# A delta-rule attention with a top-2 expert layer on one core: TensorE's order written out, outputs one unit behind, two triangular solves on VectorE

## The chip, the cores and the metric

The kernel runs on one core of a Trainium2 chip. The metric is device time in microseconds (us), lower is better. The core has a matrix engine (TensorE, PE in the profile, with its weight loads as PEld), a vector engine (VectorE, DVE), a scalar engine (ScalarE, ACT), a general engine (GpSimd, POOL) and an engine that starts transfers (SyncE, SP). Each engine works through its own instructions in order. Matrix results land in PSUM, which has eight banks; VectorE and ScalarE read them out.

## What is computed

The first half is a linear attention with a state matrix for each of 4 x 8 heads, 768 steps long, head size 40:

```
for t in range(S):
    y[:, :, t] = einsum('bhd,bhde->bhe', rt, state)
    Sa = einsum('bhde,bhe->bhd', state, at)
    state = state * wt[:, :, None, :] - einsum('bhd,bhe->bhde', Sa, bt) + einsum('bhd,bhe->bhde', vt, kt)
```

The second half sends each of the 3072 rows (all heads side by side, 320 wide) to two of eight experts. The choice is by noisy logits, `x@w_gate + log1p(exp(x@w_noise))*noise`; an expert is `relu(x@w1)@w2` with a hidden width of 1024, and the two results are summed with softmax weights.

## The kernel before

**Attention** is done in chunks of 64 steps. A unit n is one chunk cc of one half p of the batch (2 batch entries x 8 heads), so there are 12 x 2 = 24 units; p alternates. Four units (two chunks, both halves) are a group g; there are six groups.

What does not need the state is made for a whole group. `prepA` (L457, once for each p) builds the running product of w with a scan (L466), its inverse (Ln and Exp on ScalarE, a correction on VectorE, L469-475), scales b and a with it (L489, L491), splits them into two f16 parts (`pack`, L425) and sends them through DRAM into the operand stacks `st_ab` (L492-496; five buffers, SAB). NG (L477) has six buffers and is read by a transposition on TensorE at the end of each unit (`pgm`, L673). `prepC` (L505) does the same for k. `scoresL` (L520) multiplies a against b, ScalarE empties the block (L527), and four transfers write the strictly lower parts to DRAM (`scr`, L529). `tsolve` (L531) reads them as 128 small 32 x 32 systems, X, into one buffer (L534), masks them with a multiply (L535) and inverts them in 30 steps of one multiply and one add (L541, L542) on one engine, POOL for all six groups (`TPOOL`); the result is split into f16 parts th (L544, L545) and goes back to DRAM. `fetchB` (L564) brings a unit's share into dT.

A unit's `chain` (L620) is the serial part: split the state into `sfs` (L605, L606) and stack it (sE), add a·sE to W, split W (w1), apply dT (Q), copy Q to q, add the cross term to W, split again (w2), apply dT again (U), copy U twice into `vu` and once into `Ut` (L642-644), and form the new state Sst (L652). `pre` (L576) makes the next unit's key scores and first W, `blocks` (L585) its b and k blocks kb. `outp` (L654) forms the unit's output: turn U, two score blocks masked to P (L665), Y, and a scaling by the transposed NG (L676). `m.logits` (L102) then writes the output rows to DRAM, turns them, and multiplies with the gate weights. After 8, 16, 20, 22 and 24 units `route` (L127) ranks the rows by expert, and `scatter` (L158) writes a list entry for each row and choice with a POOL transfer (L162); the first are held until the last solve is issued (`m.sg`).

**Experts** follow (L273 and L295 hold their matmuls): for each expert a gather of its rows (L241), two matmul stages in three f32r parts, and a POOL transfer that adds to the output (L297).

A scheduler in the compiler orders each engine's instructions by a simulated time and a priority. `burst` (L433) ties the matmuls of one block together; which block comes after which on TensorE is the scheduler's choice. `chain` has a high priority (PRIO). Two zero matmuls are issued ahead of Q (`warm`, L568, ND).

PSUM: psc one bank, pst one, pacc three (W, Q, U, S, Y), pt two, pp one.

Of the kernel before, what the change touches and what calls it, by code (L numbers as in the profile page):

```python
# [41 lines left out]
class Moe:  # L42
    def __init__(s,nc,tc,ctx,aps):
        s.nc,s.tc=nc,tc
        s.wgn_d,s.nz_d,s.w1_d,s.w2_d,s.out_d=aps
# [56 lines left out]
    def logits(s,n,xt,ps,tag,bufs=(1,1)):  # L102

        nc=s.nc
        s.xw=nc.sync.dma_start(s.xd[n>=NA][128*n:128*n+128],xt)
# [267 lines left out]

class Att:
    PSC=1; PACC=3; PT=2; PPB=1
    def __init__(s,nc,tc,ctx,aps):
# [9 lines left out]
        s.psa=ec(tc.tile_pool(name="psa",bufs=1,space=PSUM)); s.psb=ec(tc.tile_pool(name="psb",bufs=1,space=PSUM)); s.ps=ec(tc.tile_pool(name="ps",bufs=1,space=PSUM))  # L386
        s.consts()
    def consts(s):
# [26 lines left out]
        nc.gpsimd.affine_select(out=s.tri,in_=s.tri,pattern=[[-1,32],[1,32]],base=0,channel_multiplier=0,compare_op=ALU.is_gt,fill=0.0)
# [41 lines left out]
    def prepA(s,p,g):  # L457
        nc=s.nc; FM=s.aps[0]
# [7 lines left out]
        nc.vector.tensor_tensor_scan(fl(Gx),w,fl(s.d1),0.0,op0=ALU.mult,op1=ALU.add)  # L466
# [415 lines left out]
```

## Time and profile before

| what | us |
|---|---|
| median of 3 runs (lowest, highest) | 1027.19 (1023.14, 1027.94) |
| the profiled execution: device time | 1021.33 |
| the profiled execution: span | 1019.5 |
| PE busy | 767.5 (75%) |
| POOL busy | 521.4 (51%) |
| DVE busy | 492.1 (48%) |
| ACT busy | 396.1 (39%) |

The span is from the first to the last instruction. A busy share is a mean over stages: the attention ends near 572 and the experts begin near 606. In a timeline row stand start, duration, engine, line, operation, output<-inputs, shapes, count, and in brackets how long the engine had been idle and what ended that. A row of busy times by stretch gives for each engine the busy time and the number of instructions, then the clock that TensorE was granted (1.00 is full), the mean busy share of the DMA engines, and GB/s.

### The profile page before, as it was taken

What the parts mean: (1) busy time and instruction counts of PE and PEld (TensorE: products, weight loads), DVE (VectorE), ACT (ScalarE), POOL (GpSimd) and SP (SyncE); (2) the same over time, 40 slices, a digit from 0 to 9 for tenths busy, and PEclk for the clock granted to TensorE, in tenths of its full rate; (3) what the DMA queues carried; (4) which work ended last, traced back from release to release, by engine and by line L of the source; (5) the groups of instructions that cost most, each with busy time, mean ns of one, the idle gap of its engine ahead of it and who ended that gap; (6) DMA issues with size and microseconds to landing.
All of it is one profiled execution on the core that took longest, in us unless ns stands there. A gap on an engine that the chain in (4) does not pass through costs nothing.

```text
span 1019.5 us, 25178 instructions
## 1 busy us (share of the span) xinstructions
PE 767.5 (75%) x10506; PEld 681.2 (67%) x10506; DVE 492.1 (48%) x961; ACT 396.1 (39%) x816; POOL 521.4 (51%) x678
## 2 busy tenths in 40 slices
PE   0110117687877687899799379999999999999995
PEld 0110116576666576787688259899999989999995
DVE  9329525355567556447355542643434334443430
ACT  2213213354444344554454322543434334343421
POOL 6259979237967728818874335133333333333313
PEclk9999999797778787999899779999999999999998
DMA  3799963478479557655355843426262525262303
GB/s 96 188 203 226 242 172 90 116 197 225 127 193 241 146 121 204 175 152 146 96 120 148 272 119 68 131 49 150 49 150 49 150 49 149 50 149 51 36 7 40
DMA packets 135264, 136.21 MB, mean 134 GB/s; under 512 B 67392, under 2 KB 114948, under 8 KB 135060
## 3 DMA queue, kind: packets, MB, share of 16 engines
q1 hardware_dynamic: 123492, 117.35, 43.6%
q0 software_dynamic: 11648, 17.15, 9.6%
q8 instruction: 85, 1.39, 0.6%
q14 instruction: 39, 0.32, 0.1%
HBM read 96.48 MB, written 41.37 MB: 135 GB/s over the span
## 4 chain that ended last, share of the span: by engine, by line
PE 43%; POOL 21%; DMA 14%; issue 8%; DVE 6%; SPq 3%; ACT 3%; POOLq 0%; DVEq 0%; ACTq 0%
PE po L295 16%; PE ph L273 12%; POOL Tt L541 7%; POOL X L542 7%; PE pY L441 2%; PE psc L441 2%; PE pW L441 2%; DMA X<-scr 2%; DMA xr<-xd,le 2%; DMA out_dram<-y,le 2%; DMA d_ab<-pk 2%; DMA rawk<-in_fm_dram 2%; PE pt L254 2%; POOL rawk L515 2%; POOL xr L241 1%
## 5 line engine op out<-in xcount | busy, mean ns | idle before, releaser
L297 POOL DMA_INDIRECT out_dram<-y,le x56 | 92.4, 1651 | 201.2 <-ACT y L296 171.9
L276 DVE SCALAR_TENSOR_TENSOR hl<-ph,hh 128x256 fp32r<-128x256 f32 (+1 forms) x128 | 71.0, 556 | 154.0 <-ACT hh L274 153.6
L274 ACT ACTIVATE hh<-ph 128x320 fp32r<-128x320 f32 (+1 forms) x128 | 66.1, 518 | 156.1 <-PE ph L273 155.9
L541 POOL TENSOR_TENSOR Tt<-X 128x30 f32<-128x30 f32 (+9 forms) x180 | 108.8, 604 | 11.8
L542 POOL TENSOR_TENSOR X<-X,Tt 128x30 f32<-128x30 f32 (+9 forms) x180 | 106.3, 590 | 12.6
L241 POOL DMA_INDIRECT xr<-xd,le x56 | 54.0, 965 | 74.4 <-DMA le<-ls 27.9
L441 PEld LDWEIGHTS <-st_ab 120*64 120x64 f16 (+1 forms) x928 | 26.5, 117 | 75.8 <-issue 42.2
L295 PE MATMUL po<-w2h,hh 128*128 128x320 f32 x384 | 74.6, 314 | 0.0
L441 PE MATMUL pQ<-w,dT 128*128 128x40 f16 x1152 | 41.2, 184 | 42.3 <-DMA dT<-scr 33.5
L273 PE MATMUL ph<-xh,w1h 128*128 128x512 f32 (+1 forms) x256 | 71.3, 362 | 0.5 <-ACT xh L257 0.5
L441 PEld LDWEIGHTS <-dT 128*128 128x128 f16 x1152 | 38.2, 100 | 49.6 <-DMA dT<-scr 34.4
L273 PE MATMUL ph<-xh,w1l 128*128 128x512 f32 (+1 forms) x256 | 69.0, 351 | 0.0
L273 PE MATMUL ph<-xl,w1h 128*128 128x512 f32 (+1 forms) x256 | 68.6, 349 | 0.0
L295 PE MATMUL po<-w2l,hh 128*128 128x320 f32 x384 | 68.3, 312 | 0.0
L295 PE MATMUL po<-w2h,hl 128*128 128x320 f32 x384 | 68.1, 309 | 0.0
L441 PE MATMUL psc<-st_ab 120*64 120x64 f16 x384 | 12.6, 215 | 68.1 <-DMA st_ab<-d_ab 29.6
L295 PEld LDWEIGHTS po<-w2h,hh 128*128 128x128 f32 x384 | 61.3, 188 | 3.1
L441 PE MATMUL psc<-RV,uT 128*64 128x128 f32 x384 | 56.5, 294 | 4.1 <-DVE P L665 3.7
L295 PEld LDWEIGHTS po<-w2h,hl 128*128 128x128 f32 x384 | 59.2, 188 | 0.1
L295 PEld LDWEIGHTS po<-w2l,hh 128*128 128x128 f32 x384 | 58.9, 188 | 0.4
L162 POOL DMA_INDIRECT ls<-ent,po x48 | 47.2, 984 | 19.3 <-issue 13.6
L441 PE MATMUL psc<-RV 128*64 128x128 f32 x384 | 56.6, 294 | 0.0
(285 smaller groups left out, 1893.9 us busy)
## 6 DMA issues: line engine op xcount, KB each, us to landing
w2r<-in_w_dram SPq DMA_DIRECT2D x8, 1280.0 KB
RV<-in_rv_dram SPq DMA_DIRECT2D x48, 192.0 KB
rawba<-in_fm_dram SPq DMA_DIRECT2D x24, 360.0 KB
d_ab<-pk SPq DMA_DIRECT2D x24, 360.0 KB
st_ab<-d_ab SPq DMA_DIRECT2D x36, 240.0 KB
w1r<-in_w_dram SPq DMA_DIRECT2D x8, 1024.0 KB
raww<-in_fm_dram SPq DMA_DIRECT2D x12, 365.6 KB
st_ab<-d_ab SPq DMA_DIRECT2D x24, 180.0 KB
```

What stands on the lines that cost most here:

```text
L162: st=nc.gpsimd.indirect_dma_start(out=s.ls[s.half],out_offset=OFFS(ap=po[:,j,k:k+1],axis=0),in_=s.ent[:,j,k],in_offset=None)
L241: for k in range(c,c+a): nc.gpsimd.indirect_dma_start(out=x[:p,k],out_offset=None,in_=s.xd[w],in_offset=OFFS(ap=li[:p,k,0:1],axis=0))
L254: for t,p in tiles(t0,n): nc.tensor.transpose(pt[:,t-t0:t-t0+p],x[:p,t//128,f0:f0+128],s.idm[:p,:p])
L273: for i,(a,b) in enumerate(mm): nc.tensor.matmul(ph[:,:n],a,b,start=i==0,stop=i==7)
L274: nc.scalar.activation(hh[:,f,:n],ph[:,:n],AF.Relu)
L276: if c.stop>c.start: nc.vector.scalar_tensor_tensor(o,ph[:,c],0.0,hh[:,f,c].bitcast(F32),op0=ALU.max,op1=ALU.subtract)
L295: nc.tensor.matmul(po[:p],h[:,f,r],w[:,f],start=k==0,stop=k==23); k+=1
L297: st=nc.gpsimd.indirect_dma_start(out=s.out_d,out_offset=OFFS(ap=idx[:p,ii],axis=0),in_=y[:p],in_offset=None,compute_op=ALU.add)
L441: def mm(s,*a,**k): return lambda: s.nc.tensor.matmul(*a,**k)
L515: k1=k_[:,:,:,64*b:64*b+64]; (nc.vector if g in MK else nc.gpsimd).tensor_tensor(k1,k1,G['NH'].rearrange("p (a c b) t->p b c a t",a=3,c=CG ...
L541: eng.tensor_tensor(t,Xt[:,j:j+1,j+1:].to_broadcast([128,j,m]),Xt[:,0:j,j:j+1].to_broadcast([128,j,m]),op=ALU.mult)
L542: s.tl=eng.tensor_tensor(Xt[:,0:j,j+1:],Xt[:,0:j,j+1:],t,op=ALU.add)
```

## The change

1. **TensorE's order.** `burst` ties each matmul of attention and routing to the one before it, over the whole attention. `chain`, `pre`, `outp` and `logits` are replaced by one function `slot(n)`, which writes the order out. Slot n holds unit n's serial part and, between its steps, pieces of others: the output of unit n-1, key scores, state stack, blocks and first W of unit n+1, the turned rows and logits of unit n-2, and in some slots the scores or the decay transposition (`gamma`) of a coming group. There are 27 slots. The zero matmuls (`warm`) go.
2. **Turned apart.** `blocks` is called twice, for b and for k at two places; `scoresL` is called for one chunk at a time.
3. **Routing.** `route` becomes `route1` (the choice, issued behind the slot by `choose`) and `route2` (ranks and list, issued in a later slot by `places`).
4. **VectorE's preparation in halves.** Most steps of `prepA` and the second step of `pack` are issued as two half-size instructions; so are both steps of th.
5. **Two solves on VectorE.** `TPOOL` is (2,3,4,5), so groups 0 and 1 are solved on VectorE, group 0 ahead of everything. The mask is a select on POOL for all groups. Group 1's preparation on VectorE is put behind the first solve's last step (`Behind`).
6. **Buffers and places.** psc has two banks and takes pst's; kb and sD have three buffers; the second copy of U into vu moves from VectorE to ScalarE; the state is split at the end of the slot that forms it; prepA is issued eight units ahead instead of seven, and after the slot; r and v are fetched in `fetchR`, after the slot.

```diff
+class Behind:
+    def __getattr__(s,name):
+        f=getattr(s.eng,name)
+        def g(*a,**k):
+            i=f(*a,**k)
+            s.tc.add_manual_dep(i.ins,s.first.ins.name,mybir.DependencyInfo(mybir.DependencyClass.NoSync,mybir.DependencyReason.DATA),reason="behind")
+            return i
+        return g
...
+    PSC=2; PACC=3; PT=2; PPB=1
...
+            if s.pel is not None: s.tc.add_manual_dep(i.ins,s.pel.ins.name,mybir.DependencyInfo(mybir.DependencyClass.NoSync,mybir.DependencyReason.DATA),reason="order")
+            s.pel=i
...
+        nc=s.nc; FM=s.aps[0]; V=Behind(s.tc,nc.vector,s.tl) if g==1 else nc.vector
...
+        for q in H: V.tensor_tensor(NH[:,q],P[:,q],r0[:,q],op=ALU.mult)
...
-        eng.tensor_tensor(Xt,Xt,s.tri,op=ALU.mult)
+        nc.gpsimd.affine_select(out=Xt,in_=Xt,pattern=[[-1,32],[1,32]],base=0,channel_multiplier=0,compare_op=ALU.is_gt,fill=0.0)
...
+    def slot(s,n,O,x,m,sc):
...
+        o,oP,oN=O.get(n),O.get(n-1),O.get(n+1)
+        if o:
+            p,cc,W,vu=o['G']['p'],o['cc'],o['W'],o['vu']; first=cc==0; last=cc==NG*CG-1
...
+            if not first: s.burst([s.mm(W[64*b:64*b+64,h],o['a'](h,b),o['sE'][:,b,h],start=False,stop=False,skip_group_check=True) for h,b in HB()])
+            w1=s.split320("w1",W,IS)
+        if oP: s.scores(oP,0)
+        if sc: s.scoresL(*sc,0)
+        if n-2 in x: x[n-2]['xT']=m.turned(x[n-2]['xt'],s.ps,"pt",s.PT)
+        if sc: s.scoresL(*sc,1)
+        if o:
+            Q=s.psb.tile([128,8,40],F32,name="pQ",tag="pacc",bufs=s.PACC)
+            s.apply(Q,dT,pr(w1,0),pr(w1,1),True,True)
+            q=s.wk.tile([128,8,40],F32,name="q",bufs=1); nc.scalar.activation(q,Q,AF.Copy)
+        if oN:
+            s.keys(oN)
+            if oN['cc']: oN['sD']=s.turned(oN['G']['p'])
+        if o:
...
+            s.burst([s.mm(W[64*b+32:64*b+64,h],o['lo'][r(b),h],q[r(b),h],start=False,stop=True,skip_group_check=True) for h,b in HB()])
+            w2=s.split320("w1",W,IS)
+        if oP: s.scores(oP,1)
+        if o:
+            U=s.psb.tile([128,8,40],F32,name="pQ",tag="pacc",bufs=s.PACC)
+            s.apply(U,dT,pr(w2,0),pr(w2,1),True,True)
+            for b in (1,0): nc.scalar.activation(vu[64:128,b],U[64*b:64*b+64],AF.Copy,scale=-IS)
+            nc.scalar.activation(s.Ut[:,:,0:40],U,AF.Copy,scale=-IS)
+        if oN and oN['cc']: oN['sE']=s.estack(oN['G']['p'])
+        if oP: s.gates(oP)
+        m.places(s.ps,"pp",s.PPB)
+        if n-2 in x: m.logits(n-2,x[n-2]['xT'],s.ps,"pp",s.PPB)
+        if o and not last:
...
+            s.burst(f+[s.mm(Sp[64*b:64*b+40,h],o['kb'][:,b,h],vu[:,b,h],start=False,stop=True,skip_group_check=True) for h,b in HB(1)])
+            s.split(p)
+        if o: s.uturned(o)
+        if oN: s.blocks(oN,(0,))
+        if oP:
+            s.outp(oP); x[n-1]={'xt':oP['xt'][:,0:DM]}
+            m.put(n-1,x[n-1]['xt'])
+        if sc: s.gamma(sc[0])
+        if oN: s.blocks(oN,(1,)); s.sums(oN)
...
+          with s.tc.high_priority(offset=PT_ if g else BURST):
...
+        sc={1:(1,0),2:(1,1)}
+        for g in range(2,NG): n=max(4*g-LS,3); sc[n]=(g,0); sc[n+1]=(g,1)
+        for n in range(N+3):
...
+            with s.tc.high_priority(offset=PRIO): s.slot(n,O,x,m,L)
+            m.choose()
+            if L and p:
+                prepT(g)
+                if g==NG-1: m.sg=s.tl.ins
+            if 1<ga<NG and qa<2: prepA(ga,qa)
+            if 0<gc<NG and qc<2: s.prepC(grp[gc][qc])
+            fB(n+2); fA(n+2)
+            if 0<n<N-1: s.fetchR(O[n+1])
...
-LA=7; LC=4; RB=3
+LA=8; LC=4; RB=3; LS=6
-TPOOL=(0,1,2,3,4,5)
+TPOOL=(2,3,4,5)
...
-KBB=2
+KBB=3
```

More of the change, by code (lines that the diff above doesn't have):

```diff
@@ L465, in prepA @@
         fl=lambda z: z.rearrange("p a b->p (a b)")
[L466 removed]
+        H=[slice(0,NS//2),slice(NS//2,NS)]; w3=w.rearrange("p (a b)->p a b",a=NS)
+        for q in H: V.tensor_tensor_scan(fl(Gx[:,q]),fl(w3[:,q]),fl(s.d1[:,q]),0.0,op0=ALU.mult,op1=ALU.add)
         P=Gx[:,:,1:65]
@@ L563, in fetchA, with fetchR @@
         return o
+    def fetchR(s,o):
+        n,cc,p=o['n'],o['cc'],o['G']['p']; rv=s.RV[n%2]
+        for j in range(2): s.nc.sync.dma_start(rv[64*j:64*j+48,j:j+2].rearrange("p x i b t->p (x i b t)"),s.aps[3][p,cc,j])
+        o['v'],o['r'],o['rr']=rv[:,1],[rv[:,0],rv[:,2]],rv[:,0::2]
     def fetchB(s,o,scr2):
@@ new lines, in scores, with gates @@
+    def scores(s,o,b):
+        nc=s.nc
+        pp=s.psa.tile([128,4,2,64],F32,name="psc",tag="psc",bufs=s.PSC)
+        s.burst([s.mm(pp[64*j:64*j+64,i],x[:,i,b],o['rr'][:,:,i,b],start=True,stop=True) for i in range(4) for j,x in ((1,o['uT']),(0,o['v']))])
+        m=s.wk.tile([128,8,64],F32,name="P",bufs=2)
+        nc.vector.tensor_tensor(m,pp.rearrange("p i j t->p (i j) t"),s.mk.to_broadcast([128,8,64]),op=ALU.mult)
+        o['P'].append(m)
+    def gates(s,o):
+        nc=s.nc; xt=o['xt']=s.wk.tile([128,360],F32,name="xt",bufs=2)
+        pg=s.ps.tile([128,360],F32,name="pgm",tag="pp",bufs=s.PPB)
+        s.burst([s.tp(pg[:,120*hh:120*hh+120],o['ng'][:,hh],s.idf[:120,:120]) for hh in range(3)])
+        nc.scalar.activation(xt.rearrange("p (a g e)->p a g e",a=3,g=3),pg.rearrange("p (a e g)->p a g e",a=3,g=3),AF.Copy,scale=-(2.0**-12))
@@ L699, in run @@
         gate=(s.sd0,s.sl)
         s.prepC(grp[0][0],gate)
-        with after(s.sl.ins): fA(0)
+        with after(s.sl.ins): fA(0); s.fetchR(O[0])
         s.prepC(grp[0][1],gate)
-        with after(s.sl.ins): fA(1)
-        s.pre(O[0]); s.blocks(O[0]); fB(0); fB(1)
-        with after(xd),(after(tl) if TG else ExitStack()):
-            prepA(1,0); prepA(1,1); prepT(1)
-        if m is not None:
-            with after(xd),(ExitStack() if 0 in MG else after(pl)): m.consts2(s.dm.bitcast(F32))
@@ L731 @@
-LA=7; LC=4; RB=3
+        with after(s.sl.ins): fA(1); s.fetchR(O[1])
+        s.keys(O[0]); s.blocks(O[0]); s.sums(O[0]); fB(0); fB(1)
+        with after(xd): prepA(1,0); prepA(1,1)
+        with after(xd),(ExitStack() if 0 in MG else after(pl)): m.consts2(s.dm.bitcast(F32))
+        sc={1:(1,0),2:(1,1)}
+        for g in range(2,NG): n=max(4*g-LS,3); sc[n]=(g,0); sc[n+1]=(g,1)
+        for n in range(N+3):
+            ga,qa=divmod(n+LA,4); gc,qc=divmod(n+LC,4)
+            L=None
+            if n in sc:
+                g,p=sc[n]
+                if p==0: scr[g]=s.dr.tile([2,4,CG,8,1024],F32,name="scr")
+                L=grp[g][p],p,scr[g]
+            with s.tc.high_priority(offset=PRIO): s.slot(n,O,x,m,L)
[7 more added lines that the diff above has]
+            if 0<n<N-1: s.fetchR(O[n+1])
+            if ZN<n<=ZN+4:
+                with after(m.xw.ins): m.zero(n-1-ZN)
```

262 lines of the change are left out of this document (105 added, 157 removed).

## The prediction, made before the changed kernel ran

> **What bounds the kernel now.** I read the busy time of each engine by stretches first, then the timelines of the engines that solve and of ScalarE, and the waits last. All times are us of the one profiled execution: span 1019.5, device time 1021.3, so 1.8 lie around the span. Columns: stretch, then busy time and (instructions) of PE, PEld, DVE, ACT, POOL, then granted clock, DMA share, GB/s.
>
> ```profile
> 0.00:56.00 56.00, 4.18 (x88) 3.80 (x88) 32.19 (x55) 12.35 (x19) 21.82 (x71) 1.00 0.59 150
> 56.00:149.00 93.00, 9.55 (x175) 7.93 (x176) 50.56 (x49) 22.40 (x35) 75.64 (x87) 1.00 0.88 218
> 149.00:236.00 87.00, 62.06 (x1441) 52.86 (x1441) 43.98 (x69) 37.39 (x85) 50.07 (x69) 0.87 0.54 136
> 236.00:316.00 80.00, 64.15 (x1323) 53.77 (x1321) 44.05 (x66) 36.40 (x81) 61.77 (x85) 0.80 0.72 185
> 316.00:403.00 87.00, 64.94 (x1364) 54.84 (x1361) 51.99 (x113) 37.14 (x87) 53.21 (x79) 0.81 0.69 176
> 403.00:462.00 59.00, 54.20 (x1369) 46.56 (x1368) 29.23 (x51) 30.98 (x75) 31.06 (x51) 0.99 0.64 159
> 462.00:524.00 62.00, 54.76 (x1307) 47.21 (x1307) 34.45 (x95) 28.37 (x71) 51.92 (x88) 0.92 0.46 117
> 606.00:1019.00 413.00, 397.89 (x2426) 368.96 (x2424) 161.58 (x307) 158.98 (x289) 139.11 (x105) 0.99 0.36 82
> ```
>
> The last row is the expert stage: TensorE is busy for 398 of 413 and the change does not touch it. Before it lies attention. From 56 to 149 TensorE has 10 us of work in 93: everything waits for the first solve, on POOL. After that come groups of four units. The stretches from 149 on end where the state of units 4, 8, 12, 16 and 20 is written: 87, 80, 87, 59, 62. The slow groups have the lower clock. What paces them is the solve of each group; below are the first multiply of a solve (L535) and the instruction behind its end (th, L545).
>
> ```profile
> 56.39 2.12 POOL L535 TENSOR_TENSOR X<-X,tri 128x1024 f32<-128x1024 f32 x1 [23.87 <-DMA X<-scr]
> 137.92 1.30 DVE L545 SCALAR_TENSOR_TENSOR th<-X,th 128x1024 f16<-128x1024 f32 x1 [1.85 <-ACT th L544]
> 144.27 2.12 POOL L535 TENSOR_TENSOR X<-X,tri 128x1024 f32<-128x1024 f32 x1 [1.19 <-DMA X<-scr]
> 186.23 1.49 DVE L545 SCALAR_TENSOR_TENSOR th<-X,th 128x1024 f16<-128x1024 f32 x1 [8.57 <-ACT th L544]
> 222.74 2.14 POOL L535 TENSOR_TENSOR X<-X,tri 128x1024 f32<-128x1024 f32 x1 [8.63 <-DMA X<-scr]
> 284.07 1.30 DVE L545 SCALAR_TENSOR_TENSOR th<-X,th 128x1024 f16<-128x1024 f32 x1 [1.77 <-ACT th L544]
> 295.09 2.32 POOL L535 TENSOR_TENSOR X<-X,tri 128x1024 f32<-128x1024 f32 x1 [1.53 <-DMA X<-scr]
> 353.59 1.30 DVE L545 SCALAR_TENSOR_TENSOR th<-X,th 128x1024 f16<-128x1024 f32 x1 [4.77 <-ACT th L544]
> 384.64 2.13 POOL L535 TENSOR_TENSOR X<-X,tri 128x1024 f32<-128x1024 f32 x1 [2.99 <-DMA X<-scr]
> 438.27 1.34 DVE L545 SCALAR_TENSOR_TENSOR th<-X,th 128x1024 f16<-128x1024 f32 x1 [0.76 <-ACT th L544]
> 459.14 2.14 POOL L535 TENSOR_TENSOR X<-X,tri 128x1024 f32<-128x1024 f32 x1 [22.33 <-DMA X<-scr]
> 498.51 1.31 DVE L545 SCALAR_TENSOR_TENSOR th<-X,th 128x1024 f16<-128x1024 f32 x1 [6.45 <-ACT th L544]
> ```
>
> A solve with its group's preparation beside it takes 61.3, 58.5 and 53.6 (groups 2 to 4, mean 57.8), the last, with little beside it, 39.4. From th to the next start pass 6.3, 36.5, 11.0, 31.1 and 20.9: the long ones are POOL waiting.
>
> ```profile
> POOL X L535 <- DMA X<-scr: 60.5, 6, 23.9
> POOL NG__2518 L477 <- PE pgm L442: 22.6, 1, 22.6
> POOL NG__5487 L477 <- PE pgm L442: 15.7, 1, 15.7
> ```
>
> POOL's order held a write that needs a late TensorE transposition (22.6 and 15.7 us); the other wait is the scores that feed X.
>
> **Part 1, the first solve goes to VectorE.** Removed: 60 POOL steps that POOL shares with preparation, from 56.4 to 137.9. Added on VectorE: 60 tensor_tensor over 9,920 elements a partition (twice the sum of j(31-j)). The trace has no such solve on VectorE; the nearest rows, then POOL's:
>
> ```profile
> 581.13 0.29 DVE L305 TENSOR_TENSOR fz<-acc 128x128 f32<-128x128 f32 x1
> 15.87 0.95 DVE L489 TENSOR_TENSOR rawba<-rawba,NH 120x768 f32<-120x768 f32 x1
> 162.33 0.61 POOL L541 TENSOR_TENSOR Tt<-X 128x240 f32<-128x240 f32 x1
> 91.33 1.33 POOL L541 TENSOR_TENSOR Tt<-X 128x240 f32<-128x240 f32 x1
> 10.17 1.25 POOL L415 TENSOR_SCALAR_AFFINE_SELECT tri<-tri 128x1024 f16<-128x1024 f16 x1
> ```
>
> The first two give a line of 0.16 + 0.00103 per element: 60 x 0.16 + 9,920 x 0.00103 = 19.8, and 0.04 between dependent steps makes 22. Bounds: 15 if steps overlap, 41 at POOL's pace. The mask multiply (2.1) becomes a select on POOL: 1.25 by the row, at most the old 2.1. X is there at 56.4 as now (halved preparation and two psc buffers may win or lose 3). So the solve ends at 56.4 + 1.3 + 22 = 79.7 and th's VectorE part starts at 80.5, not 137.9. From th to ScalarE's q of unit 0 now takes 12.0:
>
> ```profile
> 149.96 0.44 ACT L635 ACTIVATE q<-pQ 128x320 f32<-128x320 f32 x1 [12.07 <-PE pQ L441]
> 220.69 0.43 ACT L635 ACTIVATE q<-pQ 128x320 f32<-128x320 f32 x1
> 515.66 0.44 ACT L635 ACTIVATE q<-pQ 128x320 f32<-128x320 f32 x1 [1.19 <-PE pQ L441]
> 560.76 0.44 ACT L644 ACTIVATE Ut<-pQ 128x320 f32<-128x320 f32 x1 [0.74 <-DVE vu L643]
> ```
>
> Those are units 0, 4 and 20, and the U of unit 23. Unit 0's q moves from 150.0 to about 92.5: **57 us gained**.
>
> **Part 2, group 1 waits behind it.** prepA(1) on VectorE is now behind the first solve (Behind), and the second solve is VectorE's too. Queued behind on that engine: both preparations of group 1, those of group 2, and the units' own work. The stretches 56 to 236 hold 94.5 us of VectorE (50.56 + 43.98); some 23 of it are group 3's preparation and unit 4, not needed yet. With two solves VectorE has 71.5 + 44 = 115.5 from 57.7 on, so without a gap the second solve ends at 173; a gap of 10% makes it 184, group 2's preparation put after the solve 158. I take 170, th at 171, unit 4's q at 183 instead of 220.7. Of the 57 us about **38 stay**. TensorE waits here whatever its order is: slot 1 asks for scores of group 1, whose operands come through DRAM some 25 us after the first solve.
>
> **Part 3, groups 2 to 5.** The solve stays on POOL. One X buffer remains, so a period is: solve with what lies beside it, then th, X's load, the select. Scores of group g stand in slots 4g-6 and 4g-5, before TensorE waits for group g-1's solve; the preparation is issued eight units ahead and after the slot whose transposition it needs. So the waits of 36.5, 31.1 and 20.9 go; I take 8 for the turnaround (rows: 6.3 and 11.0), and 57.8 - 0.8 = 57 for the solve: 65 per period, 50 for the last (39.4 plus some 3 of K's multiplies, plus 8). th runs 171, 236, 301, 366, 416 against 498.5. Bounds: 58 a period if POOL's other work fits into the turnaround, 73 if the old turnarounds half return.
>
> What is late next is TensorE's slot. It has to average 65/4 = 16.2. Fast units of now show the work, together with one eviction of w:
>
> ```profile
> 450.23 0.48 DVE L652 SCALAR_TENSOR_TENSOR Sst<-pS,gam 128x320 f32<-128x320 f32 x1
> 462.01 0.49 DVE L652 SCALAR_TENSOR_TENSOR Sst<-pS,gam 128x320 f32<-128x320 f32 x1 [0.69 <-PE pd L442]
> 443.04 0.44 ACT L598 ACTIVATE w<-pW 128x320 f16<-128x320 f32 x1
> 443.51 0.49 DVE L599 SCALAR_TENSOR_TENSOR w<-pW,w 128x320 f16<-128x320 f32 x1 [1.08 <-ACT w L598]
> 554.00 0.45 PE L570 MATMUL pQ<-dm,idh 128*128 128x320 f16 x2
> 554.28 0.77 PE L441 MATMUL pQ<-w,dT 128*128 128x40 f16 x24
> ```
>
> One unit is 11.8; the warm-up matmuls that go are 0.28 of it. That leaves 4.7 a slot for waits. A written order makes every late operand hold all that follows on TensorE. Most waits have work put under them: two psc blocks and px under w1, keys and turned under q, scores under w2, estack and gates under U's copies. One is bare: pl needs pgm's bank (one pp buffer), emptied by ScalarE after vu, vu, Ut and sE, some 1.5 us. With it I come to 13.5 to 15.5, just under 16.2: POOL stays the bound, narrowly.
>
> The rest has one answer. ScalarE gets the second vu copy (0.43 x 24) and has 31.0 of 59 busy in its fullest group; half-size VectorE steps add 0.07 each, eight per preparation, inside the slack; gamma, choose/places and fetchR move within a slot or one slot later, off the path until unit 19. On SP, fetchR now stands behind its slot, and its buffer is free only then; the landing has a slot to itself. DMA work is unchanged: the shares from 56 to 524 make 313 us, which between 56 and unit 20's new place at 428 is 0.84, and 0.88 is sustained for 93 us now.
>
> **The end.** From unit 20's q to unit 23's U is 45.1 now, without preparation; I leave it. q of unit 20 is 416 + 12 = 428, U at 473. From there to the end is 1019.5 - 560.8 = 458.7; output, logits and routing of the last units come in slots 24 to 26 in the same dependence, so 0 to 4 more. Span 473 + 458.7 + 2 = 934, device time 935.5. By the scatters behind the last solve (th 498.5 to the end: 521) it is 416 + 521 = 937. The median of the runs shown, 1027.2, is 5.9 above the profiled 1021.3; with as much here: **940**.
>
> **Rivals.** *Quicker*: periods of 58, second solve done at 158: th at 159, 217, 275, 333, 376, span 895, median **901**. For it: 11.8 us units exist. Against: VectorE's 115 us before the second th. Chance 0.17.
>
> *The shared port*: POOL's 240-element multiply is 0.61 alone and 1.33 beside VectorE. The last solve's POOL steps, L541 and then L542:
>
> ```profile
> 459.00:497.00 38.00, 14.53 (x30) 0.95 0.46 129
> 459.00:497.00 38.00, 15.54 (x30) 0.95 0.46 129
> ```
>
> That is 30; if half of the steps double it is 45. Of the 15 the 57.8 hold a part; I count ten more on each of three periods: **970**. VectorE's work is denser, which speaks for it; that three solves of now ran beside VectorE in under 62 speaks against. Chance 0.17. The Trainium skill, SBUF — State Buffer, section "SBUF: two separate sides", says that VectorE and GpSimd share a port pair as an exclusive lock, taken by a VectorE operation with two SBUF inputs for its whole length; the doubled row agrees with it, and by it each of the 120 new VectorE steps shuts POOL out.
>
> *Given back*: VectorE's group 1 jam lasts until 209 (138.5 of work and 10% gaps, group 3 included) and the old turnarounds of 21 to 37 return; then unit 4 stands where it stood and nothing moves: **1015 to 1030**. Chance 0.05.
>
> *Slower*: the fixed order. A handoff (ACT 0.44, DVE 0.49, releases) is some 1.3. A slot has eight; if all stand bare, it is 11.5 + 10.4 = 21.9, unit 23's U lands at 92 + 24 x 21.9 = 617, 57 later than now: **1083**. It decides from (560.8 - 92)/24 = 19.5 a slot, six of eight bare. Against it: the listed cover. Chance 0.11.
>
> **How the numbers follow.** The forecast has 0.50, and about 915 to 965 of its own. The range 893 to 990 takes in the quick case and the port and leaves out the last two rivals. 0.5% is about what a measurement tells from no change: faster 0.84, same 0.05, slower 0.11.
>
> **What would show it.** Right: q of unit 0 near 92, second th near 171, th of group 5 near 416, POOL's waits for X under 10 each, clock above 0.9 in the middle groups. Wrong: th periods under 60 (a slot or TensorE bounds), unit spacing above 19, POOL's solve steps above 0.7 us on average, or TensorE idle behind ScalarE's pgm copy for more than 2 us a slot.

## The result and the profile after

| | median us | lowest to highest | runs |
|---|---|---|---|
| before, measured beside it | 1025.16 | 1022.43 to 1027.94 | 4 |
| changed | 1054.5 | 1051.91 to 1057.65 | 4 |

The ratio is 1.029, with a 95% interval of 1.026 to 1.032. The change makes the kernel slower by 29 us where 940 was predicted. The profiled execution has a span of 1052.0.

First the busy time by stretches of the changed kernel; the columns are those of the prediction. The stretches begin and end at copies q: 97 is unit 0's q, 227 unit 4's, 300 unit 8's, 393 unit 12's, 475 unit 16's and 541 unit 20's. The four last rows are a finer cut of the 12 us ahead of unit 10's q.

```profile
97.00:227.00 130.00, 60.44 (x1213) 53.78 (x1214) 88.50 (x187) 48.23 (x102) 32.04 (x29) 0.70 0.73 185
227.00:300.00 73.00, 58.57 (x1385) 51.65 (x1383) 40.74 (x68) 37.36 (x87) 46.75 (x70) 0.87 0.63 160
300.00:393.00 93.00, 67.50 (x1383) 59.54 (x1381) 57.97 (x127) 39.26 (x93) 57.78 (x88) 0.74 0.63 167
393.00:475.00 82.00, 65.21 (x1367) 58.33 (x1361) 39.58 (x63) 34.87 (x84) 43.47 (x69) 0.76 0.64 160
475.00:541.00 66.00, 55.83 (x1258) 49.41 (x1257) 30.53 (x90) 29.09 (x74) 54.28 (x82) 0.85 0.45 111
...
336.00:339.00 3.00, 3.00 (x52) 2.89 (x50) 3.00 (x7) 1.44 (x4) 2.78 (x4) 0.50 1.00 310
339.00:342.00 3.00, 3.00 (x60) 2.87 (x59) 2.86 (x7) 1.38 (x4) 2.71 (x4) 0.50 1.01 313
342.00:345.00 3.00, 3.00 (x56) 2.97 (x56) 2.90 (x28) 0.44 (x1) 0.69 (x2) 0.50 0.96 217
345.00:348.00 3.00, 2.63 (x75) 2.21 (x71) 3.00 (x9) 1.96 (x7) 2.76 (x4) 0.72 0.91 254
```

Unit 0 comes early, as predicted: the first solve and its hand-over end at 97. Then units 0 to 4 take 130 us, and the groups behind take 73, 93, 82 and 66 where the prediction had 65, 65, 65 and 50. The granted clock of those groups is 0.74 to 0.87. The timeline of the changed kernel names the places: ScalarE's q, POOL's select of X (groups 1, 2, 4 and 5), VectorE's th, and VectorE's NH and POOL's rawk, which will be needed below.

```profile
86.72 1.34 DVE L571 SCALAR_TENSOR_TENSOR th<-X,th 128x512 f16<-128x512 f32 x2
97.08 0.42 ACT L664 ACTIVATE q<-pQ 128x320 f32<-128x320 f32 x1
156.44 1.27 POOL L560 TENSOR_SCALAR_AFFINE_SELECT X<-X 128x1024 f32<-128x1024 f32 x1
182.77 0.56 DVE L496 TENSOR_TENSOR NH<-Gx,raww 120x384 f32<-120x384 f32 x1 [5.96 <-POOL rawk L539]
212.46 1.94 POOL L539 TENSOR_TENSOR rawk<-rawk,NH 120x384 f32<-120x384 f32 x2 [21.11 <-DMA rawk<-in_fm_dram]
214.44 1.03 DVE L496 TENSOR_TENSOR NH<-Gx,raww 120x384 f32<-120x384 f32 x2 [5.38 <-POOL rawk L539]
215.38 0.72 DVE L571 SCALAR_TENSOR_TENSOR th<-X,th 128x512 f16<-128x512 f32 x1
221.97 1.60 POOL L560 TENSOR_SCALAR_AFFINE_SELECT X<-X 128x1024 f32<-128x1024 f32 x1 [1.46 <-DMA X<-scr]
227.51 0.44 ACT L664 ACTIVATE q<-pQ 128x320 f32<-128x320 f32 x1 [6.13 <-PE pQ L464]
379.58 1.27 POOL L560 TENSOR_SCALAR_AFFINE_SELECT X<-X 128x1024 f32<-128x1024 f32 x1 [20.25 <-DMA X<-scr]
468.84 1.27 POOL L560 TENSOR_SCALAR_AFFINE_SELECT X<-X 128x1024 f32<-128x1024 f32 x1 [18.72 <-DMA X<-scr]
541.45 0.44 ACT L664 ACTIVATE q<-pQ 128x320 f32<-128x320 f32 x1 [0.37 <-PE pQ L464]
590.34 0.44 ACT L677 ACTIVATE Ut<-pQ 128x320 f32<-128x320 f32 x1
```

Set against the rows of before, unit 0's q is 53 us earlier (97.1 for 150.0), unit 4's 7 us later (227.5 for 220.7), unit 20's 26 later, the last U 30 later, the end 32 later. So the whole prologue gain is gone by unit 4, and units 4 to 20 add 19 more: 314 us for 16 units, 19.6 each, where before took 295 and the prediction had 245. What TensorE waited for from 60 to 620 us (engine, instruction, who released it, us in total, times, longest):

```profile
PE pQ L464 <- DMA dT<-scr: 80.0, 2, 46.5
PE pl L115 <- ACT xt L713: 31.3, 19, 3.1
PE pQ L464 <- DVE w L624: 14.7, 9, 3.4
```

46.5 us are one wait: unit 4 for the second solve. The 31.3 are the bare wait that the prediction priced at 1.5 a slot (1.65 on average here).

### The profile page after: what moved, and what is told of

Read it like the earlier page. It is cut to its first block, busy times and chain, and to the rows that moved or that the text cites. A ratio compares the mean times of both kernels' runs of the same rounds, so it can differ in the third digit from the quotient of the medians.

```text
span 1052.0 us, 25142 instructions
## 1 busy us (share of the span) xinstructions
PE 780.6 (74%) x10458; PEld 706.6 (67%) x10458; DVE 528.6 (50%) x1149; ACT 404.7 (38%) x846; POOL 427.2 (41%) x554
## 3 DMA queue, kind: packets, MB, share of 16 engines
q8 instruction: 84, 1.38, 0.6%
## 4 chain that ended last, share of the span: by engine, by line
PE 47%; DMA 11%; POOL 9%; DVE 6%; ACT 4%; issue 4%; SPq 1%; POOLq 0%; ACTq 0%; DVEq 0%
PE po L306 16%; PE ph L284 14%; PE psc L464 3%; POOL X L567 3%; PE pY L464 2%; POOL Tt L566 2%; PE pW L464 2%; DMA rawk<-in_fm_dram 2%; PE pt L265 2%; PE pQ L464 2%; DMA xr<-xd,le 2%; POOL xr L252 2%; DMA dT<-scr 1%; DMA X<-scr 1%; ACT vu L676 1%
## 5 line engine op out<-in xcount | busy, mean ns | idle before, releaser
L308 POOL DMA_INDIRECT out_dram<-y,le x56 | 92.5, 1651 | 201.2 <-ACT y L307 171.9
L464 PE MATMUL psc<-RV,uT 128*64 128x128 f32 x384 | 67.0, 331 | 8.2 <-DVE uT L468 7.7
L567 POOL TENSOR_TENSOR X<-X,Tt 128x30 f32<-128x30 f32 (+14 forms) x120 | 69.1, 576 | 8.5
L566 POOL TENSOR_TENSOR Tt<-X 128x30 f32<-128x30 f32 (+14 forms) x120 | 66.1, 551 | 7.8
L464 PE MATMUL psc<-RV 128*64 128x128 f32 x384 | 67.1, 332 | 2.2 <-issue 2.2
L464 PEld LDWEIGHTS psc<-RV,uT 128*64 128x64 f32 x384 | 53.7, 170 | 10.0 <-DVE uT L468 7.8
L467 ACT ACTIVATE kb<-ptr 64x320 f32<-64x320 f32 x96 | 41.2, 429 | 46.8 <-PE ptr L464 46.0
L306 PEld LDWEIGHTS po<-w2l,hh 128*128 128x128 f32 x384 | 58.9, 188 | 0.4
```

The costliest lines, as they stand in the source:

```text
L306: nc.tensor.matmul(po[:p],h[:,f,r],w[:,f],start=k==0,stop=k==23); k+=1
L308: st=nc.gpsimd.indirect_dma_start(out=s.out_d,out_offset=OFFS(ap=idx[:p,ii],axis=0),in_=y[:p],in_offset=None,compute_op=ALU.add)
L464: def mm(s,*a,**k): return lambda: s.nc.tensor.matmul(*a,**k)
L467: if e: s.nc.scalar.activation(o,i,AF.Copy)
L566: eng.tensor_tensor(t,Xt[:,j:j+1,j+1:].to_broadcast([128,j,m]),Xt[:,0:j,j:j+1].to_broadcast([128,j,m]),op=ALU.mult)
L567: s.tl=eng.tensor_tensor(Xt[:,0:j,j+1:],Xt[:,0:j,j+1:],t,op=ALU.add)
```

## The experiments

Theory A at the start: TensorE's written order leaves waits bare, the clock falls behind them, and slots are long for that. Theory B: results of VectorE and POOL come late because each works through its own order, and TensorE stands behind them. A row has the line numbers of its own kernel, which differ by a few. The median of before was 1023.6 to 1025.2 in the measurements up to g_all. Beside the six runs after that it was 1073, some 48 us more. In the traces of these six, one slot between 450 and 590 us takes 51 to 59 us (the last section shows it). They are compared by their ratio to before; an equal loss on both sides pulls such a ratio towards 1.

**Zero matmuls back into the order (a_warm).**

```diff
+    def warm(s,t,k,z):
+        s.burst([s.mm(t,s.idh,s.dm,start=z,stop=z,skip_group_check=True) for _ in range(k)])
...
+            s.warm(W,4,False)
...
+            s.warm(Q,4,True)
             s.apply(Q,dT,pr(w1,0),pr(w1,1),True,True)
...
+            s.warm(U,4,True)
```

> The changed kernel with multiplications by a zero matrix put back into TensorE's written order: four of 320 columns ahead of each Q product, four ahead of each U product, four added to W at the start of each slot (12 per slot, 24 slots). Theory A (after a stretch in which the written order leaves TensorE half idle, its granted clock stands at 0.5 for some 10 us, and the slot's own matmuls then take twice as long): the clock between 227 and 541 us rises from about 0.8 to over 0.9, the slots of 18 to 26 us shrink towards 16 to 18, and the time falls by 20 to 60 us, to 995-1035. Theory B (the slots are late because the in-order work of VectorE and POOL gives its results late; the clock only follows): the clock may rise but the slots keep their length or grow by the 12 extra matmuls (12 x 0.14 to 0.28 us = 1.7 to 3.4 us per slot where nothing hides them): 1050-1100.

Measured: 1084.7, ratio 1.061 (1.053 to 1.068), 30 us slower than the changed kernel. The clock from 227 to 461 is 0.81 where the changed kernel has 0.77. The time is on theory B's side: in an order written out, matmuls that stand ahead of a waiting one run at once and then the wait goes on, and they cost 1.9 us a slot where nothing waits (15.5 for 13.6). Theory A's clock of over 0.9 never came about, so this run does not tell what a full clock would be worth.

**Gates ahead of U (a_gates).**

```diff
-        if oP: s.scores(oP,1)
+        if oP: s.scores(oP,1); s.gates(oP)
...
-        if oP: s.gates(oP)
```

> The changed kernel with the three gate transposes (pgm) and their copy to xt moved ahead of the U product, so that the single pp bank is empty when the logits (pl) and places (pr) come. It takes away the wait of pl behind xt that the changed kernel shows 19 times with 31.3 us in all up to 620 us, and nothing else. Theory A, in the form that this wait starts the low clock: 31 us of wait and part of the low clock go, 1000-1030. Theory B (the longest idle stretches are those behind VectorE's preparation): under 15 us are gained, 1037-1055, and the clock between 227 and 541 us stays near 0.8.

Measured: 1010.3, ratio 0.986 (0.979 to 0.993): 44 us less than the changed kernel, from three transposes moved past U. pl waits for ScalarE's xt no more, and undisturbed slots go from 13.6 to 11.9. Up to unit 4 only 1.6 us are won; from unit 4's q to unit 20's it is 29 (285.2 for 313.9; the rows stand under Part 3 below). There TensorE waits 55 us for 67, since waits behind VectorE's w have grown from 11 to 24 while the 24 at pl went, and it is busy for 230 us where the same 5376 matmuls took 247. So 17 of the 29 are busy time, won at a clock of 0.84 for 0.80: theory A's time is met, and its reason in part (the clock from 227 to 461 is 0.83 for 0.77). What is left shows in the windows of three us of this run, then in VectorE's timeline around the same place.

```profile
302.00:305.00 3.00, 2.87 (x72) 2.60 (x73) 0.00 (x0) 0.82 (x2) 2.50 (x5) 1.00 0.87 242
305.00:308.00 3.00, 0.00 (x0) 0.00 (x0) 0.00 (x0) 0.11 (x1) 0.00 (x0) 1.00 0.98 258
308.00:311.00 3.00, 0.00 (x0) 0.00 (x0) 0.00 (x0) 0.00 (x0) 0.48 (x1) 0.61 0.94 174
311.00:314.00 3.00, 0.00 (x0) 0.00 (x0) 1.51 (x2) 0.00 (x0) 2.84 (x5) 0.50 0.84 211
314.00:317.00 3.00, 0.00 (x0) 0.00 (x0) 3.00 (x6) 0.00 (x0) 2.28 (x3) 0.50 0.70 254
317.00:320.00 3.00, 2.96 (x58) 2.51 (x59) 3.00 (x4) 0.88 (x2) 3.00 (x3) 0.50 0.56 222
320.00:323.00 3.00, 3.00 (x35) 2.53 (x30) 3.00 (x5) 1.17 (x2) 2.96 (x3) 0.50 0.45 127
323.00:326.00 3.00, 0.89 (x25) 0.80 (x22) 3.00 (x5) 0.77 (x2) 2.81 (x3) 0.50 0.00 0
326.00:329.00 3.00, 3.00 (x49) 2.24 (x47) 1.64 (x3) 2.93 (x8) 1.15 (x2) 0.50 0.34 64
329.00:332.00 3.00, 3.00 (x86) 2.83 (x83) 2.67 (x5) 2.83 (x7) 1.84 (x3) 0.97 0.67 171
```

```profile
300.34 0.49 DVE L720 TENSOR_TENSOR xt<-pY,xt 128x320 f32<-128x320 f32 x1 [1.12 <-PE pY L464]
312.49 1.83 DVE L496 TENSOR_TENSOR NH<-Gx,raww 120x384 f32<-120x384 f32 x2 [11.66 <-POOL rawk L539]
...
316.51 0.48 DVE L624 SCALAR_TENSOR_TENSOR w<-pW,w 128x320 f16<-128x320 f32 x1
```

VectorE stands 11.7 us at NH. Its buffer is free only when POOL has multiplied the keys (rawk) of a group before with it, and POOL waits for the load of rawk. The split w of the unit is queued behind NH, and TensorE stands at Q for 12 us; the clock falls meanwhile and is at 0.50 until about 329. This is a head-of-line wait: with LA 8 a group's prepA is written just ahead of the prepC whose result its buffer needs. The kernel before (LA 7), the changed kernel, a_gates and c_lc5 show that wait from 60 to 560 us so, a fence for each:

```profile
DVE NH L472 <- POOL rawk L515: 3.6, 1, 3.6
```

```profile
DVE NH L496 <- POOL rawk L539: 23.7, 6, 6.0
```

```profile
DVE NH L496 <- POOL rawk L539: 40.6, 7, 11.7
```

```profile
DVE NH L496 <- POOL rawk L539: 1.0, 1, 1.0
```

One wait of 3.6 us has become six and seven; with the keys a slot earlier, the next experiment, one of 1.0 is left.

**Keys one slot earlier, alone and with the gates (c_lc5, g_lc5).**

```diff
-LA=8; LC=4; RB=3; LS=6
+LA=8; LC=5; RB=3; LS=6
```

(At n=0 the calls of prepC for 4 and 5 are both made.)

> The changed kernel with the preparation of the keys (prepC: load of rawk, its product with NH on POOL, pack) one slot earlier (LC 5 in place of 4), so that it is written ahead of the next group's prepA, whose NH takes the buffer that it reads. In the changed kernel VectorE stands at NH behind POOL's rawk, and that behind rawk's load (6.0 and 5.4 us in the second solve, 9.7 us in three places of 227 to 461 us; in a_gates 28.0 us in four places, the longest 11.7), with the slot's own w, P and ak queued behind it. Theory B (these stalls of VectorE idle TensorE and so also bring the low clock): most of VectorE's waits for POOL's rawk go, the clock between 227 and 541 us rises, and 20 to 50 us are gained: 1005-1035. Theory A (the pl wait alone sets the slots and the clock): within 10 us of the changed kernel, 1045-1065.

> The gates ahead of U (run a_gates, 1010) and the keys' preparation one slot earlier, together. If the two waits are separate and both bare (theory A and B side by side): 965-990, slots 4 to 15 down from 18-25 us to 14-18. If the clock and the DMA queues set the slots anyhow, and the stall moves to the next late result (POOL's NG, dT): 1000-1015.

Measured: alone 1038.4, ratio 1.014 (1.009 to 1.020), 16 us less; with the gates **989.3, ratio 0.965 (0.960 to 0.971)**, 21 us below a_gates. In g_lc5 the wait at NH is 3.2 us, once, and the clock from 227 to 461 is 0.86. Alone the two edits win 44 and 16 us, together 65, so both waits are bare and each adds its own; the pl wait is the larger. This version beats both kernels.

**NG on VectorE (g_lc5_mg).** `MG=(1,2,3,4,5)`.

> As g_lc5, and the NG product of groups 1 to 5 on VectorE in place of POOL, so that VectorE's next scan (Gx, one buffer) doesn't wait for POOL behind its solve (13.2 and 2.5 us in the changed kernel). Ten products of 0.8 to 1.6 us go to VectorE (8 to 16 us), of them the two of group 1 in the crowded stretch. Theory B (head-of-line waits of VectorE on POOL are what is left): 5 to 15 us under g_lc5. Rival (VectorE is already full beside the slots, 58% busy in 227 to 461 us): equal or up to 15 us over g_lc5.

Measured: 995.4, ratio 0.971 (0.965 to 0.978): no gain over g_lc5; the intervals overlap. There was little left to win: in g_lc5 VectorE's waits for POOL's NG have shrunk to 1.4 and 1.3 us from the 13.2 and 2.5 of the changed kernel.

**Which engine solves (a_pool1, a_pool01, b_dve0).** `TPOOL=(1,2,3,4,5)`; `TPOOL=(0,1,2,3,4,5)` with no `Behind`; and in the kernel before `TPOOL=(1,2,3,4,5)` with top priority for the first solve.

> The changed kernel with group 1's solve on POOL again, the first solve still on VectorE. Theory B (group 1's preparation and solve on VectorE behind the first solve form a jam of 47 us for the solve and 46.5 us of waiting of TensorE at unit 4): POOL's solve, 57 us from the select at about 156, ends at 213 as VectorE's did (209), but VectorE is free, so slots 1 to 3 are shorter; second th at 205-220, time 1025-1055. Theory A (TensorE's slots at a low clock set the pace from unit 4 on): no change beyond 10 us, 1042-1062.

> The changed kernel with all six solves on POOL and group 1's preparation no longer ordered behind the first solve: the written TensorE order, the halves and the parting of routing alone. If the two VectorE solves brought the first 53 us and kept them (theory A: the loss lies in the slots behind), this run is slower than the changed kernel by 30 to 55 us: 1080-1110, with the first q at about 150 and slots as long as before. If they brought nothing in the end (theory B: what they win at unit 0 they give back by unit 4), the time is within 15 us of the changed kernel: 1040-1070, with unit 4's q near 225-240.

> The kernel before with one part of the change alone: its first solve on VectorE and at the top priority (the other five on POOL, no written TensorE order, no halves). By the prediction's first step q of unit 0 comes 50 to 57 us earlier (93-100 instead of 150), and since POOL is then free, group 1's solve can begin as soon as its scores are there. If the gain stays (theory: the old order carries it): 975-1000. If it is given back because group 1's th waits on its preparation, which now stands behind VectorE's solve: 1005-1030.

Measured: 1064.8, ratio 1.040 (1.033 to 1.047); 1070.9, ratio 1.049 (1.042 to 1.056); 1017.5, ratio 0.994 (0.991 to 0.997). The second VectorE solve is worth 10 us, both together, with `Behind`, 16, though the first alone moves unit 0's q from 130 to 97: the rest is lost by unit 4 (243 in a_pool01). a_pool1 ends 10 us above what theory B gave it (up to 1055), a_pool01 at the upper end of it (1070). In the kernel before, the same solve brings 0.6%: it runs from 57 to th at 128, and its trace has four preparations between the steps (NH at 73, 86, 97 and 116). In the changed kernel `Behind` keeps them off, and the first solve takes 29; taking `Behind` alone out of it was not tried.

**Group 1's scores ahead of slot 0 (a_pool01_sc on top of a_pool01; g_all with the gates and the keys too).**

```diff
-        sc={1:(1,0),2:(1,1)}
+        score(1,0); score(1,1); prepT(1)
+        sc={}
```

> Run a_pool01 (written TensorE order, all solves on POOL, group 1's preparation not ordered behind the first solve; 1071) with one thing changed: group 1's scores and its solve are written ahead of slot 0 in place of slots 1 and 2. In a_pool01 group 1's operands st_ab were asked for by 90 and 105 us and TensorE stood 70 us, until 129, for dT; the scores ran at 141 to 157 and POOL, free at 119, selected X only at 166. Theory (the written place of group 1's scores is what gives the prologue's gain back): X is selected right behind the first solve, at 119-125, the second th comes at 180-190 instead of 231, unit 4's q at 190-200 instead of 243, and 30 to 45 us of that stay at the end: 1025-1040. Rival (the slots behind set the end, POOL's later solves come no earlier): 1055-1075.

> All that helped together: gates ahead of U, keys' preparation one slot earlier, all solves on POOL, group 1's scores ahead of slot 0. Against g_lc5 (989): its q of unit 0 at 96 becomes about 130, its unit 4 at 222 becomes 190-200. If unit 4 sets the end: 960-970. If from there POOL's solve (57 to 65 us a group) or the slots (15 to 23 us) win only part of it: 970-985.

Measured: 1053.6, ratio 1.028 (1.021 to 1.035), 17 us below a_pool01; g_all 993.1, ratio 0.970 (0.963 to 0.976). X of group 1 is selected at 133 instead of 166 and unit 4's q is at 208 instead of 243 (198 in g_all): the theory's places are met within 9 us, its time is not (1025 to 1040): the run ends at the edge of its rival, and X of group 2 came at 227 only. g_all lies above both of its cases. In g_all unit 4 is 24 us ahead of g_lc5 and unit 8 level with it (290.6 and 290.7): X of group 2 comes at 212, behind the slots that hold its scores. The gain moves down the line and is lost there.

**Group 2's scores one slot earlier (g_all2, g_all2b, one kernel twice).** `n=max(4*g-LS,2)` for 3.

> Run g_all (993) with group 2's scores one slot earlier (slots 2 and 3 in place of 3 and 4). In g_all unit 4's q came at 198, 24 us ahead of g_lc5, but X of group 2 was selected only at 212 (217 in g_lc5), behind slots 3 and 4, and unit 8's q came at the same time (291) as in g_lc5. Theory (the written place of a group's scores sets when its solve can start, and so the group's first unit): X of group 2 at 186-195, its th at 250-260, unit 8's q at 262-275; 10 to 25 us of it stay at the end: 967-985. Rival (the preparation isn't ready either, and the wait only moves from POOL's X to TensorE's scores): X at 205-215, unchanged time, 985-1000.

> Run g_all2 again, as it is, beside g_lc5_b1 on one chip: in its first run all kernels of that call, the one before among them, lost some 45 us in one place between 455 and 570 us, where POOL issued 32 indirect transfers and TensorE waited on its own instruction issue. Its trace had X of group 2 at 195, th at 256, unit 8's q at 275 and unit 17's at 435. If that stretch is the chip's and not the kernel's: 970-985 here, ratio to before 0.95-0.96. If it belongs to this kernel's order: 1020-1040.

Measured: ratio 0.966 (0.958 to 0.973) and 0.966 (0.961 to 0.971). X of group 2 at 195, th at 256, unit 8's q at 275, as the theory had it; unit 16's q is at 423 and 427, against 435 in g_all and g_lc5. Of the 16 us at unit 8, 8 to 12 are left at unit 16. Between units 18 and 19 both traces then have one slot of 58 us, and the ratio at the end doesn't tell this kernel from g_lc5. The time of g_all2b, 1037.8, lies in the case that lays that slot to this kernel's order; before took 1073.7 beside it, so the slot is not this kernel's alone.

**The zero matmuls of before left out (b_nowarm).** `ND=(0,0,0,0)` in the kernel before.

> The kernel before with its two zero matmuls ahead of each Q product left out (ND all zero), nothing else. If they hold TensorE's clock up (then their removal is a part of the changed kernel's loss): the clock between 227 and 541 us falls and the time rises by 8 to 25 us, 1032-1050. If they don't: within 6 us of before, 1018-1030, since one pair takes 0.28 us at full clock, 24 pairs 7 us, most of them in waits.

Measured: ratio 1.006 (1.003 to 1.010), 6 us by the ratio and 8 by the medians, at the edge of the lower case. Their removal explains a small part of the loss at most.

**Priority for the second solve (a_burst1 in the changed kernel, g_lc5_b1 in g_lc5).** `offset=PT_ if g>1 else BURST`.

> The changed kernel with one thing changed: the second solve has the top priority that the first has, so that VectorE's order does not put group 2's preparation (NH, scan, packs) and the slots' own work between its steps. In the changed kernel its 60 products and sums took 161.8 to 209.1 us, 47 in place of the 22 to 24 that they take by their own durations, with 6.0 us at NH behind POOL's rawk inside and 5.4 behind it, ahead of th. Theory (the prediction's second step fell because of what stands between the steps): X at about 156 as before, solve in 22 to 30 us, th at 182-192, unit 4's q at 195-205 instead of 227.5; at the end 10 to 30 us stay: 1025-1045. Rival (unit 4's wait is set by the place of the scores and by full DMA queues): th after 200, time 1045-1065.

> Run g_lc5 (gates ahead of U, keys' preparation one slot earlier; 989) with the same priority for the second solve. Theory: th of group 1 at 182-192 instead of 211, unit 4's q at 195-205 instead of 222; but group 2's scores stay in slots 3 and 4, so X of group 2 comes at 200-212 instead of 217 and only 5 to 15 us reach the end: 975-985. Rival (as g_all, which won 24 us at unit 4 and nothing at unit 8): 986-996.

Measured: ratio 1.024 (1.019 to 1.029) and 0.968 (0.964 to 0.973); th of group 1 at 215.7 and 212.9, as without it. The edit left VectorE's order in that stretch almost as it was, so these two tell nothing of the theory; the next run asks it again.

**Group 2's preparation behind the second solve (a_late2).**

```diff
-        V=Behind(s.tc,nc.vector,s.tl) if g==1 else nc.vector
+        V=Behind(s.tc,nc.vector,s.tl) if g in (1,2) else nc.vector
...
-        for g in range(2,NG): n=max(4*g-LS,3); sc[n]=(g,0); sc[n+1]=(g,1)
+        for g in range(2,NG): n=max(4*g-LS,4); sc[n]=(g,0); sc[n+1]=(g,1)
...
-            if 1<ga<NG and qa<2: prepA(ga,qa)
+            if n==2: prepA(2,0); prepA(2,1)
+            if 2<ga<NG and qa<2: prepA(ga,qa)
```

> The changed kernel with group 2's preparation ordered behind the second solve on VectorE (as group 1's stands behind the first) and written after it; its scores go from slots 3 and 4 to slots 4 and 5. In the changed kernel VectorE did 19.7 us of products and sums of the second solve between 156.4 and 217.6, beside some 22 us of group 2's preparation, 10 of slots and 11.3 of waits at NH. Theory (the second solve is late because that work stands between its steps): solve from 157-162 to 185-192, th at 186-194, unit 4's q at 198-206 instead of 227.5. Rival (the steps wait for the slots and for DMA, whatever else stands there): th after 205. The end is a separate question: X of group 2 comes later than 222 then (230-245), so unit 8 at 305-325 instead of 300, and the time 1045-1080.

Its timeline, X's select on POOL and th of group 1 on VectorE:

```profile
147.16 1.26 POOL L560 TENSOR_SCALAR_AFFINE_SELECT X<-X 128x1024 f32<-128x1024 f32 x1 [17.98 <-DMA X<-scr]
...
180.16 1.33 DVE L571 SCALAR_TENSOR_TENSOR th<-X,th 128x512 f16<-128x512 f32 x2
```

Measured: ratio 1.037 (1.034 to 1.041). From select to th 33.0 us where the changed kernel takes 58.9 (156.44 to 215.38): the work of group 2 between the steps, with its waits, is shown as the cause of 26 us of that. Unit 4's q came at 213 only and X of group 2 at 261, both later than expected: now slot 4's own scores of group 2 stand ahead of its Q, and TensorE waits for their operands (st_ab, 41.9 us in one wait).

## Why the prediction was wrong

**Part 1 held.** th of group 0 at 86.7 for 80.5, unit 0's q at 97.1 for 92.5. A step of 240 elements takes 0.39 to 0.41 us as the line said. The difference is in the main one stall of 5.0 us that was not counted: VectorE stood at wg, a split of the router's weights that waits for a load, between two steps of the solve. A scan of group 1 (1.8 us) also came between the last step and th.

**Part 2 failed**: "without a gap the second solve ends at 173 ... I take 170". It ended at 209 and th came at 215, 44 us late. VectorE's work was summed rightly, and the gap was not:

```profile
57.70:209.00 151.30, 64.34 (x1297) 57.16 (x1292) 114.78 (x251) 53.02 (x110) 28.37 (x18) 0.80 0.75 185
```

It was busy for 114.8 us (the third engine of the row) where the sum has 115.5, and idle for 36.5, where the prediction allows 10%. Here are VectorE's groups from 156.4 to 217.6 (line, shapes, count, busy, mean ns, idle before):

```profile
L567 DVE TENSOR_TENSOR X<-X,Tt 128x30 f32<-128x30 f32 (+14 forms) x30 | 9.9, 328 | 0.8
L566 DVE TENSOR_TENSOR Tt<-X 128x30 f32<-128x30 f32 (+14 forms) x30 | 9.8, 326 | 0.6
L499 DVE TENSOR_TENSOR NH<-raww,Gx 120x384 f32<-120x384 f32 x3 | 4.1, 1379 | 0.0
L496 DVE TENSOR_TENSOR NH<-Gx,raww 120x384 f32<-120x384 f32 x4 | 2.1, 553 | 11.3 <-POOL rawk L539 11.3
```

The solve itself is 19.7 us, as priced. Group 2's preparation stands between its steps, with 6.0 us at NH behind rawk, and 5.4 more stand ahead of th. The sum of busy times had room for that preparation before and after the solve; the order did not put it there. The other part is X, which would have to be there by 148 (170 less 22) and was selected at 156: the scores stand in slots 1 and 2, and the second half of them ran at 142 to 144, when TensorE's order came to slot 2, with no wait for their operands. From 97 to 156, before there was an X, 19 of VectorE's 59 us were idle. The sum counted VectorE's work and never asked when TensorE's order reaches the scores. The 209 of the "given back" rival (chance 0.05) came true by luck: it has group 3's work in it and 10% gaps, the trace has group 2's and the waits.

**Part 3 failed at the slot**: "With it I come to 13.5 to 15.5, just under 16.2: POOL stays the bound". Units 4 to 20 took 19.6 each, and POOL's solve bound none of these groups: th of groups 2 to 5 started 28 to 35 us ahead of the q that needs it, where the prediction has 12, and TensorE waited for dT only at units 0 and 4. (In the kernel before, th of groups 1 to 5 is 34, 12, 32, 16 and 17 ahead, so not every group was paced by its solve there either.) For X of groups 4 and 5 POOL itself waited 20.3 and 18.7 us. Here is the stretch from unit 4's q to unit 20's in the changed kernel, a_gates, c_lc5 and g_lc5, then a slot of the changed kernel with nothing in its way but pl:

```profile
227.51:541.45 313.94, 247.05 (x5376) 218.87 (x5378) 169.15 (x346) 140.65 (x336) 202.30 (x305) 0.80 0.60 151
225.94:511.18 285.24, 229.99 (x5376) 204.28 (x5378) 165.96 (x346) 139.77 (x337) 192.55 (x299) 0.84 0.63 164
226.15:532.69 306.54, 244.34 (x5376) 216.15 (x5378) 166.44 (x344) 140.43 (x335) 202.27 (x305) 0.80 0.60 151
222.51:491.56 269.05, 228.76 (x5376) 203.50 (x5378) 164.03 (x344) 139.46 (x335) 190.04 (x297) 0.85 0.65 170
541.45:555.06 13.61, 12.05 (x327) 10.79 (x325) 5.40 (x11) 6.83 (x18) 4.87 (x9) 1.00 0.30 77
```

Of the 314 us TensorE was busy for 247 and waited for 67: 15.4 of work and 4.2 of waits a slot. The prediction had 11.5 of work (11.8 less 0.28) and 2 to 4 of waits. So the term that was most mis-sized is TensorE's own work. The 11.8 was read where the clock was 0.99; here it was 0.80. At the rate of the undisturbed slot (327 matmuls in 12.05 us at clock 1.00) the 5376 would take 198, an estimate; the other 49, some 3 a slot, are time at the low clock, which the prediction put at nothing although its own rows show 0.80 and 0.81 in the slow groups.

The waits are a little above what was priced, and the bare one at pl was named and priced nearly right (24 of the 67). But "most waits have work put under them" holds for handoffs of a microsecond, not for VectorE's 1.8 to 6.0 us at NH behind a load (11.7 in a_gates). Less waiting also meant less time at the low clock: without both waits (g_lc5) this stretch loses 45 us, of which 27 are waits and 18 busy time with the same matmuls. With the keys alone the clock stays at 0.80. The sign was lost by taking the 13.6 with its bare wait as good enough: gates ahead of U and keys a slot earlier give 989, and units 4 to 20 then take 16.8 each (222.5 to 491.6).

**What the miss is made of**, at the last U (590 for 473, 117 late): 44 at unit 4 (227.5 for 183), 69 in units 4 to 20 (314 for 245), 4 behind. The end held: 48.9 from unit 20 to the last U for 45.1, and 461.7 to the end for 460.7.

**Rivals.** *Slower* was the right one in kind, with its point at 19.5 a slot: from unit 0's q to the last U are 493 us, 20.6 for each of 24, with the wait of 46.5 for the second solve in it. But not six equal handoffs stood bare; one did, and the rest is that wait, longer stalls behind VectorE, and the low clock. *The shared port*: POOL's solve steps did not lengthen. In groups 2 to 5, which POOL solves in both kernels, the adds take 0.576 us on average for 0.570 before and the multiplies 0.551 for 0.559. Some short steps of VectorE did (below).

Still open: 989 against 940. Of g_lc5's 59 us at the last U (531.8 for 473), 40 are there at unit 4. From there to unit 20 it takes 269 for 245, and by the estimate above 31 of the 269 are time at the low clock. No run isolates the clock from the waits.

## What to carry to other kernels

An engine whose order is written out stands still with whichever engine is late: before fixing the order, list for each operand not only which work lies over its wait but what its producer has queued ahead of it, loads included. A sum of busy times tells when work can be done, not when its place in a queue comes; a new chain of steps needs a place of its own (here an order behind its last step), since a priority left the order as it was. Work read from a fast stretch is priced at that stretch's clock; look at the clock of the stretch for which it is used. One single-buffered bank on a path walked 24 times was worth 44 us, more than moving both solves (16).

## What the hardware showed unexpectedly

**The clock.** In a_gates TensorE stops at 305.0, and by the mean of 0.61 from 308 to 311 the clock falls at about 308.7. TensorE is then shown busy from 317.0 to 323.5 at 0.50, stands for 2.1 us, and the clock comes back at about 329.2, 3.6 us after work began again at 325.6. The Trainium skill, TensorE: Matmul & The Clock Gate, section "Part 1: The HAM clock gate (the "warmup" mystery)", gives a window of about 3.4 us both ways. This trace agrees on the way down (3.7 us) and in the second stretch of work, but not in the first, where 6.5 us did not bring the clock back. The changed kernel's rows from 336 to 345 don't agree either: TensorE is shown busy for all of nine us, and the clock stays at 0.50 until about 346.7 (worked out from the mean of 0.72 in the next row). What sets these stretches apart is not shown.

**VectorE's short steps.** In the table above three half-size NH products take 1.38 us on average: two of them 1.84 and 1.75 us (at 185.36 and 187.53), others of their kind 0.55 (at 350.92). A copy of 120x6 (L505) took 1.79 to 1.83 us in three places, the first at 154.73, and 0.15 to 0.17 in five others; In all three POOL had begun a product shortly before (at 154.68, 259.85 and 322.84), and the copy ended 0.03 to 0.04 us after that product. The Trainium skill, SBUF — State Buffer, section "SBUF: two separate sides", says that the engine that starts first holds the shared pair for its whole instruction and the other blocks; by that rule POOL was first here, and the three copies agree with it. No run isolates it.

**Slow issue.** In the runs beside which before took 1073, TensorE waited on its own issue while POOL issued its indirect transfers of the list. From g_all2b, TensorE's waits from 440 to 520 us and a piece of its timeline:

```profile
PE pY L464 <- issue: 20.8, 16, 2.6
PE ptr L464 <- issue: 4.4, 5, 1.9
```

```profile
475.67 0.21 PE L464 MATMUL ptr<-cmb,st_k 120*128 120x40 f16 x1 [0.50 <-issue]
477.76 0.22 PE L464 MATMUL ptr<-cmb,st_k 120*128 120x40 f16 x2 [1.88 <-issue]
```

Single matmuls of 0.2 us stand 0.5 to 1.9 apart, and the profile shows nothing that they wait for. g_all, nearly the same kernel, has no such wait in its list for that stretch, though POOL issues the same 32 transfers there at the same pace (0.96 us each, from 467 to 508). So the transfers alone are not the cause. One chip gave 1024 for before in one measurement and 1073 in a later one; what differs is not known.
